# Four more chunks transposed by the DMA crossbar instead of TensorE, with their attention moved to later places in the second tile

## The chip, the cores and the metric

One core of a Trainium2 chip. The metric is the device time of one execution in microseconds (us), as a median of the runs of a kernel. A run more than 1.5% above the fastest run of its kernel is slow; ratios use fast runs alone.

In the profile PE is TensorE, ACT ScalarE, DVE VectorE, POOL GpSimd and SP SyncE; a `q` behind a name means the part of the engine that issues and waits. The DMA crossbar does a transpose as a transfer (`DMA_TRANSPOSE`). A transfer lands when its semaphore reports it done. Of the tiles, `qkX` holds k and q transposed by the crossbar, `sA` the scores, `z` the state, `ff` a PSUM result of the feed-forward layer, `ob` a finished block of the output.

## The reference

A recurrent attention (RetNet) over q, k, v of shape 4 x 8 x 768 x 64, then a gated feed-forward layer with a sigmoid over 3072 tokens:

```python
state = gamma * state + k_t (outer) v_t        # per batch and head, 768 steps
y_t   = scale * q_t @ state
x     = y as [3072, 512]
out   = (sigmoid(x @ w_gate) * (x @ w_val)) @ w_out      # 512 -> 1536 -> 512
```

## The kernel before

The recurrence is done in 24 chunks of 128 tokens: scores inside a chunk, a running state between chunks. The feed-forward layer is done in six tiles of 512 tokens (four chunks each). Tile t runs as groups of matmuls (`up` and `down`), and the attention of the next tile's chunks is set between those groups at the places of a list. The scores need k and q transposed. Chunks 0 to 11 are transposed on TensorE and evicted by ScalarE, chunks 12 to 23 by the DMA crossbar, issued from SP:

```python
def transposes(g):                             # TensorE: 8 transposes, one eviction
    tp = pa.tile([128, 2 * NP, C], BF16, tag="tp", name="tp")
    for i, x in enumerate((kn[g], qn[g])):
        for p in range(NP):
            nc.tensor.transpose(tp[:, i * NP + p, :], pair(x, p), ident)
    ...
    nc.scalar.activation(qkT[g], tp, AX.Copy)

def xbar(g):                                   # crossbar: two DMA transposes on SP
    qkT[g] = ld.tile([128, 2 * NP, C], BF16, tag="qkX", name="qkX", bufs=8)
    for i, x in enumerate((kn[g], qn[g])):
        nc.sync.dma_start_transpose(out=qkT[g][:, i * NP:(i + 1) * NP, :], in_=...)

def down(t, sm, part):
    ...                                        # the last part of a 128-row block:
    ob = ffn.tile([128, D_MODEL], F32, tag="ob", name="ob")     # three buffers
    nc.scalar.copy(ob, o)
    nc.sync.dma_start(out=out[row:row + 128, :], in_=ob)        # SP too

for t in range(NT):
    ...
    elif t + 1 < NT:
        steps = attention(t + 1)
        place = [0, 1, 3, 5, 7, 8, 10, 13, 17]
    if t == 1:
        groups[:2] = [...]                     # four groups in place of two
        place = [p + 2 for p in place]
    if t + 2 < NT:
        for g in range(4 * t + 8, 4 * t + 12):
            load_chunk(g)                      # k, q, v of a chunk, issued from POOL
    for i, group in enumerate(groups):
        if i == len(groups) - 9:
            for g in range(4 * t + 8, 4 * t + 12):
                if XBAR <= g < NG:             # XBAR = 12
                    xbar(g)
        group()
        ...                                    # steps whose place is i
```

So SP carries, in program order: the four outputs of a tile, eight crossbar transposes, the four outputs of the next tile, and so on. POOL carries the loads and, for chunks 0, 1 and from 12 on, the scaling of v.

## Time and profile before

| | before |
|---|---|
| time | 238.15 us (238.10 to 238.26, 4 runs) |
| PE busy | 227.0 us, 96% of the span |
| share of PE in the chain that ended last | 90% |
| transposes on PE / on the crossbar | 96 / 24 |
| loads: median from issue to landing, kn and qn | 9.4 and 9.6 us |

Three more from the page before, to be compared later: PE's busy share in 40 slices of the span in tenths, the clock granted to TensorE in tenths, and the chain by line.

```profile
PE   7888999999999999999999999999999999999994
...
PEclk9999999999999999999999999999999999999998
...
PE ff L250 51%; PE ff L281 25%; PE sA L168 3%; DMA vf<-in_v_dram 3%; PE y L204 2%; PE y L180 2%; PE z L190 2%; PE tp L146 2%; ACT qkT L148 1%; PE ff L301 1%; POOL vs L158 1%; PE ff L264 1%; DVE xT L212 1%; ACT ob L286 1%; POOL wg L81 0%
```

PE has no gap after the first slices, runs at full clock, and nothing but matmuls is large in the chain. The only DMA in it is the start-up load of v.

### The profile page before, as it was taken

How to read it: one execution, taken by the hardware profiler on the slowest of the kernel's cores; microseconds unless marked ns; L12 is line 12 of the kernel's file. 1: busy time of each engine (PE TensorE's matmuls, PEld its weight loads, DVE VectorE, ACT ScalarE, POOL GpSimd, SP SyncE). 2: the span in 40 equal slices, each digit the busy share in tenths (PEclk: the TensorE clock that was granted, in tenths of full speed). 3: DMA queues.
4: the chain of work that ended last, by engine and by line, in shares of the span. 5: the costliest groups of instructions: out<-in, count | busy, mean ns of one | idle time of the engine just before them, and what ended most of it. 6: DMA issues, size and time to landing. Idle time of an engine off the chain costs nothing.

```text
span 236.7 us, 4316 instructions
## 1 busy us (share of the span) xinstructions
PE 227.0 (96%) x1712; PEld 119.5 (51%) x1738; DVE 105.4 (45%) x178; ACT 90.7 (38%) x170; POOL 91.9 (39%) x110
## 2 busy tenths in 40 slices
PE   7888999999999999999999999999999999999994
PEld 7665644555555554444554445444444554444443
DVE  3468446365646741346641256641346641234300
ACT  8765334425545431344333343233334331333211
POOL 8999875686787244985311001111000000000000
PEclk9999999999999999999999999999999999999998
DMA  7999999999999999999972442012100012100022
GB/s 121 196 191 181 189 203 205 191 206 233 223 182 132 127 146 157 273 143 166 164 118 89 92 89 44 3 46 90 47 0 0 3 44 87 46 3 0 0 89 89
DMA packets 77699, 27.27 MB, mean 115 GB/s; under 512 B 65072, under 2 KB 73264, under 8 KB 77680
## 3 DMA queue, kind: packets, MB, share of 16 engines
q0 software_dynamic: 57616, 16.78, 70.6%
q1 hardware_dynamic: 19776, 10.10, 21.0%
q8 instruction: 13, 0.21, 0.4%
q10 hardware_dynamic: 288, 0.13, 0.2%
q14 instruction: 6, 0.05, 0.1%
HBM read 28.31 MB, written 6.29 MB: 146 GB/s over the span
## 4 chain that ended last, share of the span: by engine, by line
PE 90%; DMA 3%; ACT 2%; POOL 2%; issue 1%; DVE 1%; SPq 0%; ACTq 0%; DVEq 0%; POOLq 0%
PE ff L250 51%; PE ff L281 25%; PE sA L168 3%; DMA vf<-in_v_dram 3%; PE y L204 2%; PE y L180 2%; PE z L190 2%; PE tp L146 2%; ACT qkT L148 1%; PE ff L301 1%; POOL vs L158 1%; PE ff L264 1%; DVE xT L212 1%; ACT ob L286 1%; POOL wg L81 0%
## 5 line engine op out<-in xcount | busy, mean ns | idle before, releaser
L255 DVE TENSOR_TENSOR hT<-gs,ff 128x512 bf16<-128x512 f32 (+1 forms) x72 | 48.6, 676 | 73.6 <-PE ff L250 70.7
L250 PE MATMUL ff<-xT,wg 128*128 128x512 bf16 (+1 forms) x276 | 71.5, 375 | 0.9 <-DVE xT L212 0.3
L250 PE MATMUL ff<-xT,wv 128*128 128x512 bf16 (+1 forms) x282 | 71.8, 375 | 0.4
L254 ACT ACTIVATE gs<-ff 128x512 f32<-128x512 f32 (+1 forms) x72 | 42.3, 588 | 68.8 <-PE ff L250 68.3
L281 PE MATMUL ff<-wo,hT 128*128 128x512 bf16 x268 | 62.4, 379 | 0.6 <-issue 0.2
L250 PEld LDWEIGHTS <-wv 128*128 128x128 bf16 x288 | 28.2, 98 | 32.7
L250 PEld LDWEIGHTS <-wg 128*128 128x128 bf16 x288 | 26.6, 98 | 30.2 <-issue 0.8
L281 PEld LDWEIGHTS <-hT 128*128 128x128 bf16 x276 | 25.9, 98 | 30.2
L286 ACT COPY ob<-ff 128x512 f32<-128x512 f32 x23 | 13.5, 585 | 52.3 <-PE ff L281 47.0
L158 POOL TENSOR_TENSOR vs<-vf,tabv 128x512 bf16<-128x512 f32 x14 | 14.5, 1046 | 44.7 <-PE y L204 39.5
L62 POOL DMA_DIRECT2D vf<-in_v_dram x23 | 20.7, 899 | 13.8 <-DMA kn<-in_k_dram 5.7
L212 DVE TENSOR_TENSOR xT<-y,taby 128x512 bf16<-128x512 f32 x24 | 16.4, 684 | 20.3 <-PE y L204 20.2
L173 DVE TENSOR_TENSOR stA<-sA,causal 128x512 bf16<-128x512 f32 x24 | 16.5, 687 | 17.3 <-PE sB L168 17.2
L67 POOL DMA_DIRECT2D kn<-in_k_dram x23 | 20.7, 901 | 8.4 <-PE ff L250 4.3
L68 POOL DMA_DIRECT2D qn<-in_q_dram x23 | 20.4, 887 | 3.9 <-DMA wo<-in_moe_w_out_dram 2.2
L198 ACT CAST zbd<-z 64x256 bf16<-64x256 f32 x40 | 14.6, 366 | 12.7 <-PE z L190 12.4
L174 DVE TENSOR_TENSOR stB<-sB,causal 128x512 bf16<-128x512 f32 x24 | 16.3, 680 | 0.0
L148 ACT ACTIVATE qkT<-tp 128x1024 bf16<-128x1024 bf16 x12 | 12.3, 1024 | 5.4 <-PE tp L146 5.3
L158 DVE TENSOR_TENSOR vs<-vf,tabv 128x512 bf16<-128x512 f32 x10 | 8.9, 894 | 3.1 <-DMA vf<-in_v_dram 3.1
L293 PE MATMUL ff<-ident 128*128 128x128 bf16 x94 | 8.7, 260 | 1.6 <-POOL ident masks.py:199 1.6
L204 PE MATMUL y<-stA,vs 128*64 128x128 bf16 x96 | 9.7, 222 | 0.0
L204 PE MATMUL y<-stB,vs 128*64 128x128 bf16 x96 | 9.5, 221 | 0.0
(52 smaller groups left out, 121.1 us busy)
## 6 DMA issues: line engine op xcount, KB each, us to landing
vf<-in_v_dram POOLq DMA_DIRECT2D x23, 256.0 KB, 9.2
out_dram<-ob SPq DMA_DIRECT2D x23, 256.0 KB, 2.0
kn<-in_k_dram POOLq DMA_DIRECT2D x23, 128.0 KB, 9.4
qn<-in_q_dram POOLq DMA_DIRECT2D x23, 128.0 KB, 9.6
wg<-in_moe_w_gate_dram POOLq DMA_DIRECT2D x6, 256.0 KB, 6.0
wv<-in_moe_w_val_dram POOLq DMA_DIRECT2D x6, 256.0 KB, 6.6
wo<-in_moe_w_out_dram POOLq DMA_DIRECT2D x4, 384.0 KB, 10.4
kf<-in_k_dram SPq DMA_DIRECT2D x1, 256.0 KB, 3.5
```

The lines of the kernel that those rows point to most:

```text
L62: eng.dma_start(out=vf[g], in_=src(v, g))
L67: nc.gpsimd.dma_start(out=kn[g], in_=src(k, g))
L68: nc.gpsimd.dma_start(out=qn[g], in_=src(q, g))
L158: eng.tensor_tensor(vs[g], vf[g], tabv[:, g % NCH, :].unsqueeze(2).to_broadcast([C, H, D]), op=ALU.mult)
L173: nc.vector.tensor_tensor(stA[g], sc[g][0], causal4, op=ALU.mult)
L174: nc.vector.tensor_tensor(stB[g], sc[g][1], causal4, op=ALU.mult)
L204: nc.tensor.matmul(y[g][i * D:(i + 1) * D, p, :], vs[g][:, 2 * p + i, :], st[:, p, :], start=(first and p == 0), stop=True, skip_group_che ...
L212: nc.vector.tensor_tensor(xT[g // 4][:, :, col:col + C], y[g], taby[:, :, c * C:(c + 1) * C], op=ALU.mult)
L250: nc.tensor.matmul(u[:, lo:hi], w[:, kk, n1 * 128:(n1 + 1) * 128], xT[t][:, kk, lo:hi], start=(kk == 0), stop=(kk == KT - 1))
L254: nc.scalar.activation(gs[:, lo:hi], ps[0][:, lo:hi], AX.Sigmoid)
L255: nc.vector.tensor_tensor(hT[t][:, n1, lo:hi], gs[:, lo:hi], ps[1][:, lo:hi], op=ALU.mult)
L281: nc.tensor.matmul(o, hT[t][:, n1, sm * 128:(sm + 1) * 128], wo[:, n1, :], start=(n1 == 0), stop=(n1 == NFF - 1))
```

## The change

The intent: take 32 transposes off TensorE, which bounds the kernel, and give them to the DMA crossbar. Since the crossbar delivers later, the attention of chunks 8 to 11 moves to later places in the second tile (all but its last step, which goes from place 19 to 18).

```diff
-    XBAR = 12
+    XBAR = 8
@@ step_t
-        scale_v(g, nc.vector if g < XBAR else nc.gpsimd)
+        scale_v(g, nc.vector if g < 12 else nc.gpsimd)
@@ main loop
         if t == 1:
             groups[:2] = [...]
-            place = [p + 2 for p in place]
+            place = [7, 9, 9, 12, 12, 14, 14, 16, 18]
@@
-            if i == len(groups) - 9:
-                for g in range(4 * t + 8, 4 * t + 12):
-                    if XBAR <= g < NG:
-                        xbar(g)
+            if t == 1 and i == 0:
+                for g in range(8, 12):
+                    xbar(g)
+            if t > 0 and i == len(groups) - 9:
+                for g in range(4 * t + 8, min(4 * t + 12, NG)):
+                    xbar(g)
```

## The prediction

> **What bounds the kernel now.** I read the page's engine totals first, then the chain that ended last, then the groups of instructions by line, PE's waits, the DMA share by slices, and last the orders of time of the SP queue and of ACT around the second tile (55 to 100 us).
>
> ```profile
> PE 227.0 (96%) x1712; PEld 119.5 (51%) x1738; DVE 105.4 (45%) x178; ACT 90.7 (38%) x170; POOL 91.9 (39%) x110
> ...
> DMA  7999999999999999999972442012100012100022
> ...
> PE 90%; DMA 3%; ACT 2%; POOL 2%; issue 1%; DVE 1%; SPq 0%; ACTq 0%; DVEq 0%; POOLq 0%
> ```
>
> TensorE is busy 96% of the span and is 90% of the chain, so only work taken off PE, or a stall put into it, moves the time. The 16 DMA engines are full in slices 2 to 20 (6 to 118 us) and nearly idle later. That early part is where the change adds transfers.
>
> The groups and PE's waits show what can be won:
>
> ```profile
> L146 PE MATMUL tp<-ident,qn 128*128 128x128 bf16 x48 | 4.9, 227 | 0.4 <-DMA qn<-in_q_dram 0.4
> L146 PE MATMUL tp<-ident,kn 128*128 128x128 bf16 x48 | 4.9, 227 | 0.0
> L148 ACT ACTIVATE qkT<-tp 128x1024 bf16<-128x1024 bf16 x12 | 12.3, 1024 | 5.4 <-PE tp L146 5.3
> ...
> PE sA L168 <- ACT qkT L148: 2.1, 4, 1.1
> ```
>
> The 227 ns of one transpose are mostly pipeline. The chain has eight of them ("PE tp L146 x8") in 0.45 us, so 0.056 us each. The evictions cost ACT 1.02 us per chunk, with no price on the chain unless the scores wait; the last line sums those waits over the run. Of its 2.1 us only 0.3 us lies in the second tile.
>
> The SP queue and ACT in the second tile:
>
> ```profile
> 46.23 11.83 SPq L288 DMA_DIRECT2D out_dram<-ob  x4
> 67.21 1.30 SPq L153 DMA_TRANSPOSE qkX<-kn  x1
> ...
> 75.30 2.13 SPq L153 DMA_TRANSPOSE qkX<-qn  x1
> 80.31 1.23 SPq L153 DMA_TRANSPOSE qkX<-kn  x1
> 83.36 1.25 SPq L153 DMA_TRANSPOSE qkX<-qn  x1
> 86.93 9.95 SPq L288 DMA_DIRECT2D out_dram<-ob  x4
> ```
>
> ```profile
> 86.32 0.58 ACT L286 COPY ob<-ff 128x512 f32<-128x512 f32 x1 [2.81 <-PE ff L281]
> ...
> 95.94 0.59 ACT L286 COPY ob<-ff 128x512 f32<-128x512 f32 x1 [2.72 <-PE ff L281]
> ```
>
> SP issues in program order: the first tile's outputs, the transposes of chunks 12 to 15, the second tile's outputs. The last two transposes went out exactly when their data had landed: kn of chunk 15 was issued by POOL at 68.63 and took 11.7 us, qn at 69.79 and took 13.6 us. SP was then free at 84.6, 2.3 us before the first output wanted it. That output was issued at 86.93 and landed 8.6 us later, at 95.5, behind the last transpose (83.36 plus 10.4, so 93.8). There are three ob buffers, so the tile's fourth copy, at 95.94, needs that landing. The old kernel passes with 0.4 us to spare.
>
> **What the Trainium skill says.**
> - "DMA: Bandwidth & Descriptors", section "DMA Transpose (X-bar)": a plain DMA transpose goes from SP or ACT, takes two-byte types and writes SBUF. The trace agrees: 24 transposes, all from SP, bf16.
> - The same page, "Rules for kernel authors": queues of SP, ACT and POOL share the same 16 engines and interleave. The trace agrees: a transpose lands in 2.4 us (median) when no load runs (131 to 167 us), and in 8.6 to 11.8 us beside the loads of 67 to 94 us.
> - "Advanced Engine Details and Errata", section "X-Bar Transpose (TRN2)", calls transposes as fast as regular DMAs. Below I derive a cost per chunk that is a good part of a load's, so I don't take them as free.
> - "TensorE: Matmul & The Clock Gate", "Why this matters for your kernels": avoid PE gaps over about 3 us, or the clock drops to half. No gap of that kind is in this trace (granted clock 0.997), so this is untested here.
>
> **The change part by part.**
>
> Removed: 4 chunks x 8 TensorE transposes = 32 x 0.056 = 1.8 us of PE, all on the chain, and the 0.3 us wait for qkT at 62.3. Together 2.1 us. ACT also loses 4 x 1.02 us, off the chain.
>
> Moved: the steps of chunks 8 to 11 go to later places. The PE work of a place is the same, so this costs nothing if the data are there. Up and down groups last 1.73 and 1.3 us in the chain. From 57.1 us I count: scores of chunk 8 at about 72.0, of 9 at 77.4, of 10 at 81.2, of 11 at 84.6. The later scale_v frees the vf buffers later (chunk 8's at about 69), still before the load that reuses it was issued in the old kernel (73.30 for chunk 16).
>
> Added: 8 DMA transposes on SP, from 58.1 us (after the first tile's last output). Where transposes follow each other with their data present (96.97 to 108.24 us), the landings are 1.7 us apart, 3.5 us per chunk, 7 to 9 us after issue. So chunk 8 lands at about 67 to 68, 9 at 71, 10 at 75, and 11, whose loads come late, at 78 to 80. Each is 4 us or more ahead of its scores: no wait there.
>
> The cost is on the DMA engines. An estimate of the exclusive DMA time of a chunk: without transposes, kn of chunks 8 to 14 landed from 52.75 to 72.3, six chunks in 19.5 us with four outputs of about 0.84 us inside, so some 2.8 us per loaded chunk. With transposes landing every 3.5 us per chunk, kn of chunks 20 to 22 came every 5.5 us: 2.8/5.5 + X/3.5 = 1 gives X = 1.7 us per transposed chunk; the stretch from 70 to 83 us gives 2.2. From 60.7 (kn of chunk 10) to the landing of qn of chunk 15 the engines must do 5.35 loaded chunks (15 us), two outputs (1.7 us) and the transposes issued so far. In the old kernel those are about 2.35 chunks, 5.2 us: 21.9 against 22.7 us measured, so the bookkeeping closes. In the new one they are about 6.4 chunks, 10.9 to 14 us, which puts the landing of qn of chunk 15 at 88 to 91.5 instead of 83.4. Its transpose lands 8 to 10 us later, at 97 to 101, and the second tile's first output behind it at about 98 to 103, say 100.
>
> The fourth copy would start at 93.7 in the new kernel. PE can go on with one gate and value pair (1.73 us) before it needs the PSUM buffer that this copy frees, so it runs dry at about 95.4. The copy lasts 0.6 us. Landing at 100 gives a stall of 100 + 0.6 - 95.4 = 5.2 us; 97.5 gives 2.7, 103 gives 8.2. A gap over about 3 us may also cost 1 to 2 us of half clock, by the skill's rule.
>
> Sum at the middle of the estimate: 238.1 - 2.1 + 5.2 + 1 = 242.2 us. I don't trust the stall fully, since it hangs on a queue of estimates, so I weight it: about one chance in five that it does not occur (236.0), the rest between 2 and 9 us. That mean is close to 240.8, which I predict.
>
> **The rivals.**
> 1. The clean gain: loads and transposes interleave better than my bookkeeping, or loads win the engines, so the first output lands by 95. Then 32 transposes are all that changes: 236.0 us, 0.9% faster. For it: the new places leave each score 4 us of slack, as if chosen with the landings in view, and the profile charges DMA only 3% of the chain. Against it: the margin of 0.4 us at 95.9, and loads that took 11.7 to 17.9 us once the old transposes ran.
> 2. The scores wait for the crossbar: the transposes of chunks 8 to 11 start at the moment when loads are thickest (q0's packets took 160% to 180% of the engines' time between 57 and 72 us). If they come at the slower pace of the old first batch (4.5 us per chunk, last landing some 10 us after issue) chunk 11 lands at about 84 to 85 and its scores wait up to 1 us: 237 us without the output stall. Its sign would be PE sA waiting for the qkX DMA.
> 3. scale_v of chunks 12 to 15 on POOL comes too late: it stands behind the issue of vf of chunk 19 (93.64 in the old kernel), which moves by 4 x 1.9 = 7.6 us to about 101, so vs of chunk 12 is ready near 103. Its use comes at 107 minus 2. This is near, but hides behind any output stall; alone it would cost under 1 us.
> 4. The stall at full size: every transpose pays 2.2 us and the clock drops. Landing at 103, stall 8.2, clock 2: 246 us.
>
> **Range and chances.** Low end 236.0 is rival 1, high end 246.0 is rival 4; both should be reachable, so the range holds about 8 in 10. Slower by over 2% means over 242.9, a stall of about 6 us with a little clock loss: 0.33. Faster by over 2% means under 233.3, and nothing on the chain would give 4.8 us: 0.01. The rest, 0.66, is within 2%.
>
> **What would show it.** Right: 64 instead of 96 PE transposes and 8 instead of 12 ACT evictions; eight more DMA_TRANSPOSE on SP from 58 us; qn of chunk 15 transposed after 88 us; the second tile's first output issued and landed later than 86.9 and 95.5; a wait of the ob copy for out_dram near 94 to 100 us in ACT's waits, followed by idle PE at an ff group and perhaps a lower granted clock. Wrong: no such wait, the second tile ending 2 us earlier than before and that lead kept to the end (rival 1); or PE idle before sA or z (rivals 2 and 3). The whole would also be wrong if removed transposes gave less than 0.45 us per chunk.

## The result, and the profile after

The changed kernel takes 259.81 us (257.53 to 261.14, 4 runs), against 238.15. The ratio is 1.0899, 95% interval 1.0821 to 1.0976: 9% slower.

From the page of the changed kernel, PE and its clock in slices, then the chain by engine and by line:

```profile
PE   7798999999999790009999999999999999999994
...
PEclk9999999999999998555999999999999999999999
...
PE 77%; DMA 14%; POOL 4%; ACT 1%; SPq 1%; DVE 1%; issue 1%; POOLq 0%; ACTq 0%; DVEq 0%
PE ff L250 47%; PE ff L281 19%; DMA kn<-in_k_dram 9%; DMA out_dram<-ob 5%; PE sA L168 2%; PE y L204 2%; PE z L190 1%; PE y L180 1%; PE ff L264 1%; PE ff L301 1%; SPq L153 1%; PE tp L146 1%; POOL vs L158 1%; ACT qkT L148 1%; POOL vf L62 1%; POOL kn L67 1%
```

One hole in PE, in slices 16 to 18 (a slice is 6.45 us here). The granted clock falls inside it and is at half in slices 17 to 19, beyond its end: in windows it was 1.00 from 97.0 to 100.5 us and 0.50 from 101 to 116. A load of k and an output transfer have entered the chain. PE's waits and ACT's (who waited for whom, us in total, times, longest) say what the hole is:

```profile
PE ff L250 <- ACT ob L286: 19.3, 1, 19.3
...
PE sA L168 <- DMA qkX<-qn: 1.7, 1, 1.7
```

```profile
ACT ob L286 <- DMA out_dram<-ob: 22.3, 1, 22.3
```

One wait of 19.3 us. PE waits for an `ob` copy on ACT, which waits for an earlier output to leave its buffer. The chain in order of time (start, us, what) goes on from there, back to what held the output:

```profile
77.36 21.98 DMA kn<-in_k_dram
...
99.36 1.19 SPq L153
...
102.13 13.42 DMA out_dram<-ob
...
115.66 0.59 ACT ob L286
...
116.29 3.57 PE ff L250 x8
```

Read upwards: PE resumes at 116.29 when the copy is done; the copy waited for the tile's first output, issued at 102.13 and landed at 115.6. SP could not issue it before the transposes of chunk 15, and those waited for k of chunk 15, a load issued at 77.36 that took 22.0 us. That load is late twice over: it landed at 99.3 us instead of 80.3 in the kernel before, of which 10.3 us are the longer flight (22.0 against 11.7) and 8.7 the later issue (77.36 against 68.63). By the semaphores in the trace, POOL's loads take eight in turn, so a load goes out only after the one eight places earlier has landed: here q of chunk 12, at 76.8 us instead of 68.0. One slow load thus holds up those behind it. SP's own order of time shows the same queue, to be held against the SP lines in the prediction:

```profile
57.88 1.35 SPq L153 DMA_TRANSPOSE qkX<-kn  x1
...
71.39 3.12 SPq L153 DMA_TRANSPOSE qkX<-qn  x1
74.89 1.57 SPq L153 DMA_TRANSPOSE qkX<-kn  x1
...
99.36 1.19 SPq L153 DMA_TRANSPOSE qkX<-kn  x1
100.64 1.40 SPq L153 DMA_TRANSPOSE qkX<-qn  x1
102.13 14.47 SPq L288 DMA_DIRECT2D out_dram<-ob  x4
```

The transposes of chunk 15 went out at 99.36 and 100.64 (before: 80.31 and 83.36), the first output at 102.13 (before: 86.93). What the half clock costs is in PE's order of time, around the hole:

```profile
96.00 1.03 PE L250 MATMUL ff<-xT,wv 128*128 128x512 bf16 x4
116.29 1.87 PE L250 MATMUL ff<-xT,wg 128*128 128x512 bf16 x4 [19.26 <-ACT ob L286]
117.95 1.91 PE L250 MATMUL ff<-xT,wv 128*128 128x512 bf16 x4
```

The first pair after the hole takes 3.57 us in the chain instead of 1.73, and the pace is back by 121.7; with the eight scores and the next gate that is about 2.5 us more (an estimate: 5.4 us from 116.29 to 121.7 for work that takes 2.9 at full clock).

The sum closes on the two profiled spans, 236.7 and 258.0 us: -2.0 for the PE work and a short wait that goes with it (measured below), +1.7 for chunk 11's scores, +19.3, +2.5 make +21.5 against +21.3.

### The profile page after: what moved, and what is told of

It is laid out like the page before. It is cut to its first block, busy times and chain, and to the rows that moved or that the text cites. A ratio compares the mean times of both kernels' runs of the same rounds, so it can differ in the third digit from the quotient of the medians.

```text
span 258.0 us, 4296 instructions
## 1 busy us (share of the span) xinstructions
PE 228.6 (89%) x1706; PEld 117.8 (46%) x1706; DVE 104.8 (41%) x178; ACT 87.0 (34%) x166; POOL 91.9 (36%) x110
## 4 chain that ended last, share of the span: by engine, by line
PE 77%; DMA 14%; POOL 4%; ACT 1%; SPq 1%; DVE 1%; issue 1%; POOLq 0%; ACTq 0%; DVEq 0%
PE ff L250 47%; PE ff L281 19%; DMA kn<-in_k_dram 9%; DMA out_dram<-ob 5%; PE sA L168 2%; PE y L204 2%; PE z L190 1%; PE y L180 1%; PE ff L264 1%; PE ff L301 1%; SPq L153 1%; PE tp L146 1%; POOL vs L158 1%; ACT qkT L148 1%; POOL vf L62 1%; POOL kn L67 1%
## 5 line engine op out<-in xcount | busy, mean ns | idle before, releaser
L250 PE MATMUL ff<-xT,wg 128*128 128x512 bf16 (+1 forms) x288 | 74.1, 381 | 19.7 <-ACT ob L286 19.3
L255 DVE TENSOR_TENSOR hT<-gs,ff 128x512 bf16<-128x512 f32 (+1 forms) x72 | 48.6, 676 | 96.4 <-PE ff L250 68.6
L250 PE MATMUL ff<-xT,wv 128*128 128x512 bf16 (+1 forms) x288 | 73.5, 378 | 0.0
L281 PE MATMUL ff<-wo,hT 128*128 128x512 bf16 x276 | 63.1, 379 | 0.0
L62 POOL DMA_DIRECT2D vf<-in_v_dram x23 | 20.8, 904 | 35.2 <-DMA kn<-in_k_dram 19.3
L67 POOL DMA_DIRECT2D kn<-in_k_dram x23 | 20.7, 899 | 13.4 <-DMA qn<-in_q_dram 5.8
L148 ACT ACTIVATE qkT<-tp 128x1024 bf16<-128x1024 bf16 x8 | 8.2, 1025 | 1.9 <-PE tp L146 1.8
(52 smaller groups left out, 114.8 us busy)
```

Of the source, the lines that this page charges most:

```text
L62: eng.dma_start(out=vf[g], in_=src(v, g))
L67: nc.gpsimd.dma_start(out=kn[g], in_=src(k, g))
L250: nc.tensor.matmul(u[:, lo:hi], w[:, kk, n1 * 128:(n1 + 1) * 128], xT[t][:, kk, lo:hi], start=(kk == 0), stop=(kk == KT - 1))
L255: nc.vector.tensor_tensor(hT[t][:, n1, lo:hi], gs[:, lo:hi], ps[1][:, lo:hi], op=ALU.mult)
L281: nc.tensor.matmul(o, hT[t][:, n1, sm * 128:(sm + 1) * 128], wo[:, n1, :], start=(n1 == 0), stop=(n1 == NFF - 1))
```

## The experiments

**Theory A**: the added transposes slow the loads that run beside them; late loads make the transposes of chunk 15 late; they stand on SP ahead of the second tile's outputs; the fourth `ob` copy waits for the first output, and PE for that copy. **Rivals**: B, the full DMA engines slow everything, whatever waits for what; C, the moved attention, or its wait for the crossbar, is the cause.

Twelve kernels ran, each with four runs beside its kernel before (238.08 to 238.11 us). In kernels that stall on DMA the runs scatter by up to 5%, some slow; where a profile fell in such a run (four buffers, the copies in 1 KB pieces, half the dose), I use it for where the waits lie, and the ratio of fast runs for the time.

| kernel | median us (range) | ratio |
|---|---|---|
| no transposes for chunks 8 to 11 (wrong result) | 236.06 (235.94 to 237.16) | 0.9918 |
| before, new places only | 237.74 (237.72 to 238.02) | 0.9982 |
| changed, old places | 257.47 (256.19 to 259.72) | 1.0816 |
| before, 8 extra transposes | 258.87 (257.34 to 260.50) | 1.0843 |
| before, 8 extra copies, 1 KB pieces | 244.45 (240.97 to 247.20) | 1.0166 |
| before, 8 extra copies, 256-byte pieces | 245.25 (242.80 to 250.15) | 1.0256 |
| changed, chunks 10 and 11 only | 250.79 (247.56 to 253.20) | 1.0437 |
| changed, 4 output buffers | 251.03 (247.25 to 253.00) | 1.0428 |
| changed, outputs issued from ACT | 274.86 (269.83 to 279.15) | 1.1365 |
| changed, 4 buffers, v scaled on VectorE, 2 places later | 238.28 (236.25 to 248.49) | none given |
| changed, loads gated | 239.21 (238.85 to 240.18) | 1.0043 |
| changed, loads gated, 4 buffers, v scaled on VectorE | 236.27 (236.24 to 236.37) | 0.9914 |

**What the PE work is worth.** The transposes of chunks 8 to 11 left out, a wrong result:

```diff
-                    xbar(g)
+                    qkT[g] = qkT[7]
```

> The changed kernel with the transposes of chunks 8 to 11 left out and not replaced: their scores read chunk 7's transposed tile, so the result is wrong on purpose. PE has the instructions of the changed kernel, the DMA engines those of the kernel before. If the removed PE work is worth what the prediction says (32 transposes, 1.8 us, and 0.3 us of waiting) and the places cost nothing: 236.0 us. If the new places themselves hurt (the rival), more than 238.

236.06 us. And the places alone:

```diff
 # kernel before
-            place = [p + 2 for p in place]
+            place = [7, 9, 9, 12, 12, 14, 14, 16, 18]
```

> The kernel before with the new places alone, transposes of chunks 8 to 11 on TensorE as before. Theory A: places cost nothing, 238.1 us within 0.5 us. Rival (later scale of v frees the v buffers late and delays loads and outputs): the loads of chunks 16 to 19 land later and the time rises by several us.

237.74 us. So the places cost nothing; they win 0.3 us (238.08 less 237.74), as the scores of chunk 8 no longer wait for their eviction: the one such wait between 56 and 97 us, 0.3 us, is gone from the trace. So small a gain is not beyond doubt (interval of the ratio 0.9958 to 1.0006). The transposes are worth another 1.7 (237.74 less 236.06). Together 2.0 us of gain were there to be had. Rival C, as far as the places go, is out.

**Is it PE's schedule or the DMA stream that sets the end?**

```diff
 # changed kernel
-            place = [7, 9, 9, 12, 12, 14, 14, 16, 18]
+            place = [p + 2 for p in place]
```

> The changed kernel with the places of the kernel before: the scores of chunk 8 come at 61.5 us while its transposes land at 68.6, so PE waits some 7 us there. Theory A (the end is set by the DMA stream: loads of chunk 15, its transposes, the first output of the tile, landing at about 115.6 us): this wait is absorbed, the time stays at 258 to 260 us. Rival (PE sets the end and the waits add up): about 266.

257.47 us, just under the 258 to 260 expected. PE's and ACT's waits in this run:

```profile
PE ff L250 <- ACT ob L286: 11.8, 1, 11.8
PE sA L168 <- DMA qkX<-qn: 7.6, 1, 7.6
```

```profile
ACT ob L286 <- DMA out_dram<-ob: 15.5, 1, 15.5
```

PE waits 7.6 us at chunk 8 and the later hole shrinks from 19.3 to 11.8 us: what was lost early was not lost again late. The first output landed at 115.9 us here and at 115.6 in the changed kernel. The DMA stream sets that moment; PE's schedule does not.

**The transposes alone, in the kernel before.** PE keeps its own transposes; eight crossbar transposes into tiles that nobody reads are added on SP at the place of the change:

```diff
 # kernel before
+            if t == 1 and i == 0:
+                for g in range(8, 12):
+                    for x in (kn[g], qn[g]):
+                        d = ld.tile([128, NP, C], BF16, tag="spare", name="spare", bufs=8)
+                        nc.sync.dma_start_transpose(out=d, in_=x.rearrange("s h d -> s (h d)"))
```

> The kernel before, with the eight crossbar transposes of chunks 8 to 11 added at the same place on SP into tiles that nobody reads. PE's own work is that of the kernel before. Theory A (the added transposes slow the loads, everything follows from that): the first output of the second tile lands near 115 us as in the changed kernel, and the time is 257 to 260. Rival (it is the moved attention and its wait for the qkX of chunk 11 that start it): near 238.

258.87 us, with the same hole. PE's wait and ACT's:

```profile
PE ff L250 <- ACT ob L286: 19.6, 1, 19.6
```

```profile
ACT ob L286 <- DMA out_dram<-ob: 23.3, 1, 23.3
```

No attention was moved and no score depends on the added transposes: rival C is out entirely.

**Bytes, pieces, or the transposing?** The same addition as plain copies from SBUF to SBUF, first in rows of 1 KB:

```diff
-                        nc.sync.dma_start_transpose(out=d, in_=x.rearrange("s h d -> s (h d)"))
+                        nc.sync.dma_start(out=d.rearrange("s p c -> s (p c)"), in_=x.rearrange("s h d -> s (h d)"))
```

> The same with eight plain copies of the same bytes from SBUF to SBUF in place of the eight transposes. If it is the bytes and the place in the queue that cost, it is as slow as with extra transposes (257 to 260). If it is the transposing (more and slower packets beside the loads), the loads of chunk 15 land a few us later than in the kernel before (83 us), the outputs stall little, and the time is 238 to 244.

then into a padded tile, so that the copies move in 256-byte pieces, 512 each, about as many as a transpose has (528 packets for each copy in the trace, 544 for a transpose, 144 for a copy in 1 KB rows):

```diff
+                        d = ld.tile([128, NP, C + 16], BF16, tag="spare", name="spare", bufs=8)
+                        nc.sync.dma_start(out=d[:, :, :C], in_=x.rearrange("s (p i) d -> s p (i d)", i=2))
```

> The kernel before with eight plain copies added as in the earlier run, but into a padded tile, so that they move in pieces of 256 bytes, 512 of them each, as a transpose does. If the number of small packets is what costs: as slow as the extra transposes, 257 to 260, loads of chunk 15 landing near 103 us. If it is the crossbar: as the plain copies in 1 KB rows, 241 to 247, loads of chunk 15 near 88.

244.45 and 245.25 us, both by the rule at 2% unclear (intervals 1.0098 to 1.0234 and 1.0197 to 1.0315), but far from the 258.87 with transposes. The number of pieces hardly matters. The first median lies just above the 238 to 244 I had set; its two fast runs, 240.97 and 243.46, lie within. The load of q of chunk 15, issue plus landing time, came down at 87.7 us with the 1 KB copies (71.64 + 16.1), at 88.3 with the small pieces (73.2 + 15.1), and at 103.5 with the transposes (79.5 + 24.0); it was 83.3 in the kernel before. The DMA issues of these three runs, in windows around that load (size, us to landing), first with extra transposes, then 1 KB copies, then 256-byte pieces:

```profile
qn<-in_q_dram POOLq DMA_DIRECT2D x1, 128.0 KB, 24.0
```

```profile
qn<-in_q_dram POOLq DMA_DIRECT2D x1, 128.0 KB, 16.1
```

```profile
qn<-in_q_dram POOLq DMA_DIRECT2D x1, 128.0 KB, 15.1
```

A plain copy of the same megabyte delays this load by 4.4 to 5 us, the transposes by 20. It is transposing beside loads that is expensive: between 66 and 96 us the DMA engines of the changed kernel moved 106 GB/s and those of the kernel before 152, nearly always busy in both. Why the engines get so little done in that mix, no record here shows.

**Half the dose.** Chunks 10 and 11 alone on the crossbar:

```diff
-    XBAR = 8
+    XBAR = 10
-                for g in range(8, 12):
+                for g in range(10, 12):
                     xbar(g)
```

> The changed kernel with chunks 10 and 11 alone moved to the crossbar, 8 and 9 transposed on TensorE. Theory A with a cost in proportion: qn of chunk 15 lands half way between 83.3 and 100.0 us, near 92; the first output near 105; PE dry from about 96; about 246 to 248 us. Rival (a threshold: two chunks fit into the slack): 237 to 238.

250.79 us, somewhat above the 246 to 248 expected (fast runs 247.56 and 249.76). q of chunk 15 landed at 93.1 us, near the 92 foreseen, but the first output at 109.2, not 105. There is no threshold under which two chunks fit.

**The buffer.**

```diff
-        ob = ffn.tile([128, D_MODEL], F32, tag="ob", name="ob")
+        ob = ffn.tile([128, D_MODEL], F32, tag="ob", name="ob", bufs=4)
```

> The changed kernel with four output buffers (ob) in place of three. Theory A (the fourth ob copy of the second tile waits for the landing of the first output, which stands on SP behind the transposes of chunk 15): the 22.3 us wait of ACT for out_dram and the 19.3 us gap of PE at about 97 us go. But the scale of v of chunks 12 to 15 stands on POOL behind the load of v of chunk 19, issued at 114.9 us in the changed kernel; if the loads are no faster now, PE waits at z of chunk 12 from about 105 to 117 us instead, so about 250 us. Rival B (PE is slowed by the full DMA engines whatever waits for what): no change, 258 to 260. Rival C (the buffer was all of it): 237.7.

251.03 us. PE's waits in this run:

```profile
PE sA L168 <- DMA qkX<-qn: 6.0, 3, 4.4
PE z L190 <- POOL vs L158: 5.4, 2, 5.0
```

The wait at `ob` is gone from both engines, so rival B as stated is out. But the gain is only part of the hole, because the late loads have other victims: the scores wait for late transposes, and the state of chunk 12 waits for v, whose scaling stands on POOL behind the load of v of chunk 19. The sum is what I expected; of the 12 us at `z`, 6.0 showed up at the scores instead.

**The outputs on another queue.**

```diff
-        nc.sync.dma_start(out=out[row:row + 128, :], in_=ob)
+        (nc.scalar if t == 1 else nc.sync).dma_start(out=out[row:row + 128, :], in_=ob)
```

> The changed kernel with the second tile's four outputs issued from ACT, so that they stand behind no transpose. Theory A: the first output is issued near 84.6 us and lands near 93, the fourth copy does not wait; as with four buffers, PE then waits for the scaled v of chunk 12 to about 117 us: about 250 us, with the same wait as with four buffers. Rival B (slow outputs are slow by bandwidth alone): the output lands after 105 and PE still stalls at the ob copy.

A clear miss: 274.86 us. ACT's order of time:

```profile
84.68 0.59 ACT L286 COPY ob<-ff 128x512 f32<-128x512 f32 x1 [0.88 <-PE ff L281]
108.27 0.38 ACTq L288 DMA_DIRECT2D out_dram<-ob  x1
108.68 0.74 ACT L198 CAST zbd<-z 64x256 bf16<-64x256 f32 x2 [23.42 <-DMA qkX<-kn]
```

The copy was done at 85.3, but the output was issued at 108.27. By the semaphore events in the trace, the DMAs of SP and ACT take the same semaphores in turn, and ACT had to wait until the transpose that last used this one (k of chunk 14) landed at 108.2. That wait stood in ACT's own order, so the state copy behind it (`zbd`) was held up too, and with it PE (18.6 us in its waits, and 9.9 at `ob`). Another queue is not free of the transposes, and here the wait stood in the way of computing, which it does not on SP. By the letter the sign of rival B came (the output landed at 116.4, PE stalled at `ob`), but the output was issued 23 us late and took 8.1 us, so bandwidth alone was not it. The run neither supports nor refutes theory A.

**Removing the waits together.** Four buffers, v of chunks 12 to 15 scaled on VectorE, and the last two attention steps of the second tile later (16 to 17, 18 to 19):

```diff
-        scale_v(g, nc.vector if g < 12 else nc.gpsimd)
+        scale_v(g, nc.vector if g < 16 else nc.gpsimd)
-            place = [7, 9, 9, 12, 12, 14, 14, 16, 18]
+            place = [7, 9, 9, 12, 12, 14, 14, 17, 19]
```

with the four buffers as above.

> The changed kernel with four output buffers, the scale of v of chunks 12 to 15 on VectorE, and the last two steps of the second tile's attention one and one place later. Theory A: the waits at ob and at z (5 us of it in the run with four buffers) are gone; what is left is the wait of the scores for the crossbar (6.0 us there, 4.4 of it for chunk 11, which lands near 87 to 91 us against a use at 86 to 87 in the new place): 237 to 241 us. Rival (another queue behind the loads takes over): above 244.

Two runs of 236.3 us, one of 240.2, one of 248.5. Where the transposes come in time the whole gain is there, but it has no margin: the loads are still late. In the profiled run, one of the two fast ones, q of chunk 15 landed at 98.9 us and the first output at 112.2, and nothing waited for them any more. So what costs is not the late transfers as such, but the waits for them. What waited in the run of 248.5 us is not on record.

**The mixing itself.** The last theory to test: it is the time that transposes and loads spend together that is expensive, so loads that start later should land earlier. Nothing is removed; POOL reads two columns of the transposed tile of the group before, and so holds its next loads until those transposes have landed:

```diff
+        if t == 1:
+            for g in range(8, 12):
+                xbar(g)
         if t + 2 < NT:
+            if t > 0:
+                gate = at.tile([128, 2], BF16, tag="gate", name="gate")
+                for i in range(2):
+                    nc.gpsimd.tensor_copy(gate[:, i:i + 1], qkT[4 * t + 7][:, i * NP + NP - 1, C - 1:])
             for g in range(4 * t + 8, 4 * t + 12):
                 load_chunk(g)
-            if t == 1 and i == 0:
-                for g in range(8, 12):
-                    xbar(g)
```

> The changed kernel with one thing added: before the loads of each group of four chunks from chunk 12 on, POOL reads the last column of the transposed tile of the group before, so those loads start only when its transposes have landed. Nothing is removed. If the mixing of loads and transposes is what costs, the later start pays: chunk 11's transposes land by 75, the loads of chunk 15 near 88 to 91, its transposes near 98, the first output near 99, a stall of 4 us, then scaled v of chunk 12 near 109: 240 to 244 us. If the DMA engines simply have too much work, delaying loads makes it worse: above 260.

239.21 us: 20.6 us of the 21.7 lost come back from a pause of the loads. The load of k of chunk 15 in a window of the changed kernel, then of this one (us to landing):

```profile
kn<-in_k_dram POOLq DMA_DIRECT2D x1, 128.0 KB, 22.0
```

```profile
kn<-in_k_dram POOLq DMA_DIRECT2D x1, 128.0 KB, 9.9
```

It was issued at 80.92 us here, 3.6 us later than in the changed kernel, and landed at 90.8 instead of 99.3. POOL's and SP's order of time in the gated kernel:

```profile
72.16 0.19 POOL L414 COPY gate<-qkX 128x1 bf16<-128x1 bf16 x1 [13.03 <-DMA qkX<-kn]
```

```profile
69.45 1.75 SPq L153 DMA_TRANSPOSE qkX<-qn  x1
...
92.79 1.19 SPq L153 DMA_TRANSPOSE qkX<-qn  x1
94.07 3.36 SPq L288 DMA_DIRECT2D out_dram<-ob  x4
```

The loads pause for 13 us. The transposes of chunk 11 land at 72.5 us (87.1 in the changed kernel), and the first output goes out at 94.07 instead of 102.13 and lands 2.3 us later instead of 13.4. A wait of 1.7 us of PE at `ob` is left and one of 1.1 at `z`.

Two things are at work in this run. The mixing is one: q of chunk 15 landed at 92.8 us here and at 100.0 in the changed kernel, with the same loads and the same eleven transposes landed before it in both, so the same work was done 7.2 us sooner in spite of the pause (from 57 us on the DMA engines moved 5.3 MB in 35.7 us here, 5.5 MB in 43.0 there). The order is the other: the gate also holds back the loads of chunk 16, issued from 96.06 us on, while in the changed kernel k, q and v of chunk 16 and k of chunk 17 landed before the first output did. How the remaining 12 us of that output's lead divide between the two, no run separates.

With the gate, four buffers and VectorE's scaling of v of chunks 12 to 15 together:

> The same gate, with four output buffers and the scale of v of chunks 12 to 15 on VectorE. If mixing was the cost, nothing waits any more and only the removed transposes count: 236.0 to 237 us, as the kernel without transposes. If not: above 240.

236.27 us, ratio 0.9914, interval 0.9895 to 0.9933, all four runs within 0.13 us. From its page:

```profile
PE   7798999999999999999999999999999999999994
...
PEclk9999999999999999999999999999999999999999
```

The hole and the half clock are gone. This is the kernel without any transposes of chunks 8 to 11 (236.06) to within 0.2 us, with a correct result: the change's whole gain, and faster than both kernels, over the kernel before by less than 1%. Four buffers and the scaling on VectorE were not tried on the kernel before; that they add nothing there is likely, since the removed transposes account for the gain, but not shown.

## Why the prediction was wrong

- **The removed work**: right. 2.1 us foreseen, 2.0 measured.
- **The new places cost nothing**: right, and even 0.3 us of gain, which is the wait I had counted.
- **Each transpose lands 4 us or more ahead of its scores**: wrong for all four. Chunks 8, 9 and 10 landed at 68.6, 74.8 and 79.6 us (foreseen: 67 to 68, 71, 75), 3.1, 2.7 and 2.1 us ahead, so nothing waited. Chunk 11 landed at 87.1 us, not 78 to 80, and PE waited 1.7 us, as in rival 2, which had allowed up to 1.
- **The path of the loss**: right in every link: loads of chunk 15, its transposes on SP, the first output behind them, the fourth copy, PE at the gate of the next tile.
- **The size of the stall**: wrong, and this is the step that failed: "X = 1.7 us per transposed chunk". I took X from stretches where four chunks were transposed beside loads. Here q of chunk 15 landed at 100.0 us, not at 88 to 91.5. By the prediction's own bookkeeping, from k of chunk 10 (60.2 us) that is 39.8 us, less 15 for loads and 1.7 for outputs, over some 6.2 transposed chunks: an estimate of 3.7 us per chunk, twice X and well above the 2.2 of its upper end. One X for all mixes was the error: with the loads held back, the four transposes of chunks 10 and 11 landed 0.4 to 0.5 us apart (71.2 to 72.6 us in the gated kernel). Two slips in the sum matter little: 19.5 us less four outputs of 0.84 over six chunks is 2.7, not 2.8, and the old kernel's bookkeeping closes with the larger X (5.2 us for 2.35 chunks); with 1.7 it gives 20.7 against 22.7.
- **The transposes of chunk 15 land 8 to 10 us after issue**: wrong by the same cause. It was 14.1 us (100.64 to 114.8), and the first output landed at 115.6 instead of 100. The stall of 19.3 us instead of 5.2 is those two terms, less the 1.7 us by which PE ran dry later.
- **The clock**: right in kind (1 us put in, about 2.5 estimated from the trace). For its 1 to 2 us the prediction shows no working.
- **The weighting**: one chance in five for no stall pulled the number down to 240.8. Even unweighted it would have been 242.2.
- **Rival 3**, v scaled too late on POOL, hid behind the stall as foreseen, and took 5.0 us once the buffer was freed, not under 1.

Argued, not shown: how a transpose takes so much of the engines' time beside a load. The runs show only that it does, and that bytes and the number of pieces explain no more than a quarter of it (5 of 20 us of delay).

## What to carry to other kernels

A transfer added to full DMA queues costs what it does to the transfers beside it, and that cost depends on the mix; measure it by adding it unread to the old kernel, which took one run here. Follow each queue in program order to what stands last in it: an output behind a late transpose stopped TensorE through three buffers. Where two kinds of transfer disturb each other, holding one back until the other is done can make both earlier, as it did here.

## What the Trainium skill lacked or had wrong

- "Advanced Engine Details and Errata", section "X-Bar Transpose (TRN2)", calls transpose DMAs as fast as regular ones. Beside loads they are not: eight of 128 KB added to the old kernel moved the landing of chunk 15's q from 83.3 to 103.5 us, eight plain copies of the same size to 87.7 or 88.3.
- "DMA: Bandwidth & Descriptors", section "Rules for kernel authors", says that a transpose next to ordinary DMAs needs nothing. That is about the result, and no run here came out wrong but the one that was meant to; on the time that such a mix costs the section has nothing: holding the loads back took the changed kernel from 259.81 to 239.21 us.
